# Second layers of group 1: two blocks through all their products, then the other two

## The chip, the cores and the metric

The kernel runs on one core of a Trainium2 chip. The metric is the time of one execution on the device in microseconds (us), as the median of several runs; lower is better.

## The reference

The program has two stages. The first is a gated linear recurrence over 768 steps for 4 x 8 heads of size 48; its output, with the heads side by side, is the matrix x of 3072 rows and 384 columns. The second is a mixture of four experts over the rows of x, and the change lies in its second layer:

```python
def _moe_ref(x, domain_probs, w1, w2):
    p = domain_probs / (domain_probs.sum(-1, keepdims=True) + 1e-09)
    out = np.zeros((N, D))                 # N, D, E, F = 3072, 384, 4, 1024
    for e in range(E):
        h = np.maximum(x @ w1[e], 0.0)
        out += p[:, e:e + 1] * (h @ w2[e])
    return out
```

## The kernel before

**Blocks and groups.** The rows of x are made in 24 blocks of 128 rows, called units, each by the generator `attention(u)` (lines 273 to 479). A group is a set of units that go through the experts together: group 0 has two units, groups 1 to 5 have four, group 6 has two. For every group and expert e the kernel runs `up` once for each of the eight f-chunks (fc, 128 of the 1024 hidden features) and then `down` for the group's blocks, here called slots. The two last groups take turns expert by expert; the others go one after the other.

**Split products.** A product of two fp32 matrices is made either whole, with fp32 operands, or from parts. Line 226 and the lines after it split a weight into a top, a low and a dif part, and lines 584 to 593 do the same for the hidden activations. A sum in parts is three products with fp32r operands: part 0 (H), part 1 (L) and part 2 (D), each taking the part of that number from weight and activation. In `up`, H and L go into one bank of PSUM ("one") and D into a second ("two"). In `down`, H and L of a slot go into one bank (`side` 0 of the code), and D into another (`side` 1), and each of the two sums is added into the slot's accumulator by `add_up`, on VectorE at line 666 (scaled by `p_fine` for side 0, by `p_all` for side 1) or, for the first sum of a slot, on ScalarE at line 664.

**Group 1.** Groups 2 and later split all of w1 and w2; they read the split weights from DRAM (`kept`), where group 0 put those of w1 and group 1 those of w2. Group 1 is in between. Its first layers use split w1. Its second layers use w2 whole for e = 0. For e = 1, 2 and 3 they use parts for the first half of the f-chunks (fc 0 to 3, w2 pieces 0 and 1, split during `up`), and the whole w2 for the other half (fc 4 to 7, pieces 2 and 3). These last are split only during and after the products, for the later groups. The whole products are part 3 in the code and are summed into the same bank as D.

**Order in `down`.** A call for group 1 with e > 0 takes all four slots, in two pairs. The steps, one matmul of 128x384 each, are written out as a list: line 613 runs over the sides, then the pairs, then the kinds of products of that side. That gives 64 steps: 16 H and L products of the first pair, 16 of the second, 8 whole and 8 D products of the first pair, 8 and 8 of the second. A sum gets its bank from a ring of four (pool tag "g", shared with "one" and "two" of `up`) at its first step, and its `add_up` is issued at its last.

Three things are tied to the number n of the step, not to the product that stands there: `background()`, which takes the next piece of work for splitting w2 (every eighth step); `make_dif` (line 592), which makes the dif part of the hidden activations of an f-chunk (at n = 3, 7, 11 and 15); and `advance`, which runs attention's next pieces when a clock of estimated costs has come to their due time. Every engine has its own queue and works through it in the order in which the instructions were issued.

**Names in the profile.** L637 is `down`'s matmul: "ops<-w,hT" is a product of parts, "ops<-hT" a whole product, of which each shows as two records. L538 and L546 are matmuls of `up`, L557 ScalarE's read of "one", L559 and L564 VectorE's read of "two" (L564 for the chunks that stay whole), L596 ScalarE's ReLU for these, L584, L586 and L592 the split of the hidden activations. L226 to L232 split w2, L502, L252 and L253 split x. Of attention, L270 is a transpose ("tp", of the inputs ra, rk, rq), read by L281, L286 and L293; L312 copies queries ("qb"); L338 and L393 are its score products ("sc", "far"), L348 and L406 take them up; L319, L321, L330 and L331 go to the next level.

Of the kernel before, what the change touches and what calls it, by code (L numbers as in the profile page):

```python
# [20 lines left out]
def kernel(  # L21
# [166 lines left out]
    def load_piece(l, i, beside=False):  # L188
        if i >= E * NQ * LAST:
            return  # L190
        gi, k = divmod(i, E * NQ)
        e, c = divmod(k, NQ)
        if gi > l:
            w = wt[l][i] = wts.tile([P, 3, KC * QF], F32R, name=f"w{l + 1}",
                                    bufs=AHEAD if l == 0 else NQ)
            nc.sync.dma_start(out=w.bitcast(F32), in_=kept[l][k])
            return
        if l == 1 and not beside:
            return
        if l == 0:  # L200

            if gi > 0 or e == 0:
                shared[c] = wts.tile([P, 3, KC * QF], F32R, name="w2", bufs=NQ)
            w = shared[c][:, 2 - e % 2 if gi == 0 else 2].bitcast(F32)
        else:

            place = (hidden[c][:, 0] if not split2(gi, e, c) else hidden[c + NQ // 2][:, 1])
            w = place.rearrange("p f n -> p (f n)")[:, :KC * QF].bitcast(F32)
        wt[l][i] = w
        if l == 0:  # L210
            heads = moe_w1[e].rearrange("(h d) f -> h d f", d=D)[:, :, c * QF:(c + 1) * QF]
            w = w.rearrange("p (c f) -> p c f", f=QF)
            for part in range(2):
                nc.sync.dma_start(out=w[:, part], in_=heads[part * H // 2:(part + 1) * H // 2, :QUAD])
            nc.sync.dma_start(out=w[:, 2], in_=heads[:, QUAD:])
        else:
            nc.sync.dma_start(
                out=w.rearrange("p (c d) -> p c d", d=DM),
                in_=moe_w2[e].rearrange("(c p) d -> p c d", p=P)[:, c * FPQ:(c + 1) * FPQ])

    def split_piece(l, i):
        whole = wt[l][i]
        w = wts.tile([P, 3, KC * QF], F32R, name=f"w{l + 1}", bufs=AHEAD if l == 0 else NQ)
        top, low, dif = (w[:, part] for part in range(3))

        nc.scalar.activation(out=top, in_=whole, func=ACT.Copy, scale=TRIM)  # L226
        yield
        nc.scalar.activation(out=dif, in_=whole, func=ACT.Copy, scale=TRIM * 4096)
        yield
        nc.vector.scalar_tensor_tensor(out=low, in0=whole, scalar=4096.0, in1=dif.bitcast(F32),  # L230
                                       op0=ALU.mult, op1=ALU.subtract)
        nc.vector.tensor_sub(dif, low.bitcast(F32), top.bitcast(F32))  # L232
        nc.gpsimd.dma_start(out=kept[l][i % (E * NQ)], in_=w.bitcast(F32))
        if l == 0:
            del wt[0][i]
        elif split2(1, *divmod(i - E * NQ, NQ)):
            wt[1][i] = w

    def background():


        for piece in list(splitting):
            if next(piece, splitting) is splitting:
                splitting.remove(piece)
        if making and len(splitting) < 4:
            splitting.append(making.popleft())
            next(splitting[-1])
# [343 lines left out]
    def make_dif(top, low, dif):  # L591
        nc.vector.scalar_tensor_tensor(out=dif, in0=top.bitcast(F32), scalar=1 / 4096.0,  # L592
                                       in1=low.bitcast(F32), op0=ALU.mult, op1=ALU.subtract)
# [5 lines left out]
    def down(gi, e, slots, between):  # L599


        first = first_piece(gi, e)
        in_parts = [fc for fc in range(FCH) if split2(gi, e, fc // FPQ)]
        whole = [fc for fc in range(FCH) if fc not in in_parts]
        if slots[0] == 0 and makes[1](gi, e):
            making.extend(split_piece(1, first + k) for k in range(NQ) if not split2(gi, e, k))
        if slots[0] == 0 and makes[0](gi, e) and 0 < e < E - 1:
            making.extend(split_piece(0, first + k) for k in range(2, NQ))


        pairs = [slots[k:k + 2] for k in range(0, len(slots), 2)]
        sides = [[((0, 1), in_parts[:-2]), ((0, 1), in_parts[-2:])], [((3,), whole), ((2,), in_parts)]]
        steps = [(side, slot, part, fc) for side in range(2) for pair in pairs
                 for parts, tiles in sides[side] for part in parts for slot in pair for fc in tiles]
        begins = {key: n for n, key in reversed([*enumerate(step[:2] for step in steps)])}
        ends = {step[:2]: n for n, step in enumerate(steps)}
        sums = {}
        for n, (side, slot, part, fc) in enumerate(steps):
            c, f = divmod(fc, FPQ)
            advance(cost(1, gi, e) * len(slots) / len(steps))  # L620
            while between and n >= between[0][0] * len(steps):
                between.popleft()[1]()
            if n and n % (len(steps) // (2 * len(slots))) == 0:
                background()
            if later and n % (len(steps) // 12 - 1) == len(steps) // 12 - 2:
                make_dif(*later.popleft())
            at = (side, slot)
            if n == begins[at]:
                sums[at] = ps.tile([P, DM], F32, name="ops", tag="g", bufs=4)
            h = hidden[c][:, :, f, slot * P:(slot + 1) * P]  # L630
            if part < 3:
                w = wt[1][first + c].rearrange("p t (c d) -> p t c d", d=DM)[:, part, f]
                h = h[:, part]
            else:
                w = wt[1][first + c].rearrange("p (c d) -> p c d", d=DM)[:, f]
                h = h[:, 2].bitcast(F32)
            nc.tensor.matmul(sums[at], lhsT=h, rhs=w, start=(n == begins[at]), stop=(n == ends[at]))  # L637
            if n == ends[at]:
                add_up(gi, e, slot, side, sums.pop(at))
        while between:  # L640
            between.popleft()[1]()
        background()
        if slots[-1] == len(groups[gi]) - 1 and gi != LAST - 1:
            while makes[1](gi, e) and (making or splitting):
                background()

            for c in range(NQ):
                del wt[1][first + c]
                if c < NQ // 2 or gi == LAST:
                    load_piece(1, first + NQ + c)  # L650
                else:
                    late.append(first + NQ + c)

    def add_up(gi, e, slot, kind, part):

        cb, b = groups[gi][slot]
        at = b * NCB + cb
        if e == 0 and (kind == 0 or not split2(gi, e)):
            accs[cb, b] = hid.tile([P, DM], F32, name="acc", bufs=B) if gi < LAST else \
                work.tile([P, NP * P], F32, name="QT")[:, :DM]  # L660
        acc = accs[cb, b]
        scale = (p_fine if kind == 0 else p_all)[:, at, e:e + 1]
        if e == 0 and (kind == 0 or not split2(gi, e)):
            nc.scalar.activation(out=acc, in_=part, func=ACT.Copy, scale=scale)
        else:
            nc.vector.scalar_tensor_tensor(out=acc, in0=part, scalar=scale, in1=acc,  # L666
                                           op0=ALU.mult, op1=ALU.add)
        if kind == 0:
            return
        if e == E - 1:  # L670
            del accs[cb, b]
            row = b * S + cb * P
            stores.append(lambda: (nc.sync if gi >= LAST - 1 else nc.gpsimd).dma_start(
                out=out[row:row + P, :], in_=acc))
# [3 lines left out]
    def cost(layer, gi, e):  # L678
        n = len(groups[gi]) / 4
        if layer == 0:  # L680
            return 2.1 * n if split1(gi, e) else 2.6 * n
        return 4.1 if gi > 1 else 4.7 if split2(gi, e) else 5.4
# [32 lines left out]
    def advance(spent):  # L715
        nonlocal clock
        clock += spent
        while waiting and clock >= waiting[0][0]:
            next(waiting.popleft()[2], None)

    with tc.manual_schedule():
# [38 lines left out]
        for fc in range(FCH):  # L760
            up(0, 0, fc, slice(0, 1))
            advance(cost(0, 0, 0) / 2)
        down(0, 0, [0], deque())
        while waiting:
            next(waiting.popleft()[2], None)
# [4 lines left out]
        for (gi, e), after in zip(tasks, [*tasks[1:], (None, None)]):  # L770
# [5 lines left out]
            turns = [range(k, k + each) for k in range(rest, len(groups[gi]), each)]  # L776
# [39 lines left out]
```

## Time and profile before

| | |
|---|---|
| Time, median of 9 runs | 1066.93 us (1066.0 to 1067.85) |
| Profiled execution | 1066.0 us, of which the span is 1064.2 us |
| Busy share of the span: PE, DVE, ACT, POOL | 98%, 73%, 53%, 3% |
| Chain of work that ended last: PE, ACT, DVE | 87%, 5%, 5% |
| `down`, products of parts | 1872 records, 347.5 us busy |
| `down`, whole products | 288 records, 101.0 us busy |
| Group 1's `down` with e = 1, 2, 3 | from 236.49, 282.06 and 326.73 us |

PE is TensorE, DVE is VectorE, ACT is ScalarE, POOL is GpSimd, SP is SyncE, which issues most DMAs. Times in rows of the profile are us from the start of the span, mean durations of one instruction are in ns. In a timeline each row has the start, the duration, the engine, the line, the operation, the tiles written and read, the number of records merged into it, and in brackets the engine's idle time before it with the instruction that ended that idle time.

### The profile page before, as it was taken

Reading aid. Unit: us, or ns where it says so; the run is one execution under the profiler, and the core shown is the slowest. Engines: PE = TensorE matmul, PEld = TensorE weight load, DVE = VectorE, ACT = ScalarE, POOL = GpSimd, SP = SyncE. Lnnn points to the kernel's source line nnn. Section 1 sums busy time; section 2 is a strip of 40 time slices with the busy share of each in tenths; the row PEclk is TensorE's granted clock in tenths of the full one; section 3 lists DMA queues with packets and bytes.
Section 4 is the critical chain, followed back from the end, with each engine's and each line's share of the span. In section 5 each row is a group of like instructions: output and inputs, shape, how many; then the busy total and the mean of one; then the engine's idle time right before and its main releaser. Section 6 shows DMA issues by size and latency. Waiting matters only on the chain.

```text
span 1064.2 us, 21598 instructions
## 1 busy us (share of the span) xinstructions
PE 1041.2 (98%) x8508; PEld 905.7 (85%) x8508; DVE 781.3 (73%) x1619; ACT 569.0 (53%) x1202; POOL 32.8 (3%) x71
## 2 busy tenths in 40 slices
PE   8899999999999999999999999999999999999998
PEld 8776776687877898898898998988989889898988
DVE  5488777667769777778877877986877875656565
ACT  5687876574655555536546535555464443323232
POOL 2010000000000000000000000000000000000000
PEclk9999999999999999999999999999999999999999
DMA  8597799896878958658659558585694454444531
GB/s 123 155 321 217 242 318 349 291 345 211 309 250 282 360 174 285 272 160 326 239 192 362 199 197 335 172 310 227 172 367 177 195 208 171 185 179 178 205 151 45
DMA packets 158837, 251.66 MB, mean 236 GB/s; under 512 B 120112, under 2 KB 135344, under 8 KB 136208
## 3 DMA queue, kind: packets, MB, share of 16 engines
q1 hardware_dynamic: 149600, 208.82, 57.5%
q0 software_dynamic: 5760, 41.29, 9.6%
q8 instruction: 67, 1.10, 0.4%
q10 hardware_dynamic: 3376, 0.17, 0.3%
q14 instruction: 34, 0.28, 0.1%
HBM read 207.79 MB, written 42.47 MB: 235 GB/s over the span
## 4 chain that ended last, share of the span: by engine, by line
PE 87%; ACT 5%; DVE 5%; issue 2%; DMA 1%; SPq 0%; DVEq 0%; ACTq 0%
PE ops L637 37%; PE one L546 22%; PE two L546 11%; PE sc L338 6%; PE yps L432 3%; PE tp L270 3%; PE one L538 2%; ACT qb L312 2%; PE far L393 1%; PE sps L467 1%; DVE near L348 1%; DVE w L230 1%; DMA rq<-in_q_dram 1%; ACT KT L330 1%; DVE QT L319 1%
## 5 line engine op out<-in xcount | busy, mean ns | idle before, releaser
L637 PE MATMUL ops<-w,hT 128*128 128x384 f32 x1872 | 347.5, 340 | 0.4 <-DVE hT L564 0.4
L637 PEld LDWEIGHTS ops<-w,hT 128*128 128x128 f32 x1872 | 325.3, 188 | 4.9 <-DVE hT L564 0.7
L546 PE MATMUL one<-xT,w 128*128 128x512 f32 x960 | 253.1, 399 | 2.2 <-DVE xT L252 1.4
L546 PEld LDWEIGHTS one<-xT,w 128*128 128x128 f32 x960 | 175.8, 188 | 41.3 <-DVE xT L252 3.1
L557 ACT ACTIVATE t<-one 128x512 f32<-128x512 f32 (+1 forms) x192 | 107.2, 558 | 183.9 <-PE one L546 178.6
L312 ACT COPY qb<-QT 64x256 f32<-64x256 f32 x336 | 136.6, 407 | 73.4 <-DVE QT L293 44.8
L586 DVE SCALAR_TENSOR_TENSOR hT<-t,hT 128x512 fp32r<-128x512 f32 (+1 forms) x172 | 110.5, 642 | 68.9 <-ACT hT L584 66.6
L559 DVE TENSOR_TENSOR t<-t,two 128x512 f32<-128x512 f32 (+1 forms) x172 | 109.4, 636 | 58.7 <-ACT t L557 29.7
L584 ACT ACTIVATE hT<-t 128x512 fp32r<-128x512 f32 (+1 forms) x172 | 101.8, 592 | 86.1 <-DVE t L559 85.0
L546 PE MATMUL two<-xT,w 128*128 128x512 f32 x480 | 136.3, 392 | 0.0
L546 PEld LDWEIGHTS two<-xT,w 128*128 128x128 f32 x480 | 90.1, 188 | 20.0 <-DVE acc L666 0.2
L637 PE MATMUL ops<-hT 128*128 128x384 f32 x288 | 101.0, 492 | 3.1 <-DVE acc L666 3.1
L592 DVE SCALAR_TENSOR_TENSOR hT<-hT 128x512 fp32r<-128x512 f32 (+1 forms) x172 | 100.9, 633 | 0.0
L348 DVE COPY_PREDICATED near<-masks,sc 128x256 f32<-128x256 uint8 x144 | 76.9, 534 | 19.3 <-PE sc L338 16.5
L319 DVE TENSOR_TENSOR QT<-QT,dec 128x256 f32<-128x256 f32 x144 | 60.8, 422 | 36.0 <-ACT qb L312 35.3
L338 PEld LDWEIGHTS sc<-qb,KT 128*64 128x64 f32 x2304 | 72.7, 138 | 9.3 <-issue 4.7
L338 PE MATMUL sc<-qb,KT 128*64 128x64 f32 x2304 | 77.2, 223 | 2.6 <-ACT qb L312 2.6
L637 PEld LDWEIGHTS ops<-hT 128*128 128x128 f32 x288 | 51.9, 190 | 32.5 <-DVE acc L666 3.7
L666 DVE SCALAR_TENSOR_TENSOR acc<-ops,p_all,acc 128x384 f32<-128x384 f32 x82 | 50.0, 614 | 32.4 <-PE ops L637 31.2
L330 ACT COPY KT<-KT 128x256 f32<-128x256 f32 x144 | 60.0, 417 | 3.1
L331 DVE TENSOR_TENSOR KT<-KT,dec 128x256 f32<-128x256 f32 x144 | 60.1, 418 | 0.0
L538 PE MATMUL one<-xT,w 128*128 128x256 f32 (+1 forms) x240 | 46.2, 340 | 0.6 <-ACT xT L448 0.6
(88 smaller groups left out, 935.0 us busy)
## 6 DMA issues: line engine op xcount, KB each, us to landing
w<-kept SPq DMA_DIRECT2D x144, 1152.0 KB
kept<-w POOLq DMA_DIRECT2D x32, 1152.0 KB, 7.3
hT<-in_moe_w_dram SPq DMA_DIRECT2D x32, 384.0 KB
w<-in_moe_w_dram SPq DMA_DIRECT2D x48, 128.0 KB
ra<-in_alpha_dram SPq DMA_DIRECT2D x23, 192.0 KB
rk<-in_k_dram SPq DMA_DIRECT2D x23, 192.0 KB
rq<-in_q_dram SPq DMA_DIRECT2D x23, 192.0 KB
out_dram<-acc POOLq DMA_DIRECT2D x18, 192.0 KB, 7.6
```

What stands on the lines that cost most here:

```text
L312: nc.scalar.copy(out=qb[rows, :, i, :].rearrange("p a (b r) -> p a b r", r=m), in_=qv[rows])
L319: nc.vector.tensor_mul(qv, qv, spread(dv[:, :, :, 0], m))
L330: nc.scalar.copy(out=new[:, :, :, 1, :], in_=old[:, :, :, 1, :])
L338: nc.tensor.matmul(out[HALF * s:HALF * (s + 1), 2 * p:2 * p + 2, :], lhsT=KTs[li][:, p, HALF * s:HALF * (s + 1)], rhs=qbs[li][:, p, :, QUA ...
L348: nc.vector.copy_predicated(near.rearrange("p a (b two r) -> p a b two r", two=2, r=m)[:, :, :, 1, :], mk.unsqueeze(1).broadcast_to([P, H, ...
L546: nc.tensor.matmul(out, lhsT=w[:, part, kc], rhs=x_part(gi, part, kc), start=(part == terms[0] and kc == 0), stop=(part == terms[-1] and k ...
L557: nc.scalar.activation(out=t, in_=one, func=ACT.Copy, scale=FINE)
L559: nc.vector.tensor_add(t, t, two)
L584: nc.scalar.activation(out=top, in_=x, func=ACT.Relu, scale=TRIM)
L586: nc.vector.scalar_tensor_tensor(out=low, in0=x, scalar=0.0, in1=top.bitcast(F32), op0=ALU.max, op1=ALU.subtract)
L592: nc.vector.scalar_tensor_tensor(out=dif, in0=top.bitcast(F32), scalar=1 / 4096.0, in1=low.bitcast(F32), op0=ALU.mult, op1=ALU.subtract)
L637: nc.tensor.matmul(sums[at], lhsT=h, rhs=w, start=(n == begins[at]), stop=(n == ends[at]))
```

## The change

Where a call of `down` has whole products beside products of parts, the pairs of slots become the outer loop and the sides the inner one. The first pair goes through H and L, whole products and D, and then the second pair does the same. Only the three calls for group 1 with e = 1, 2 and 3 have whole products and two pairs, so only their order differs. All other calls keep theirs. Lines after 613 have numbers higher by two.

```diff
         pairs = [slots[k:k + 2] for k in range(0, len(slots), 2)]
         sides = [[((0, 1), in_parts[:-2]), ((0, 1), in_parts[-2:])], [((3,), whole), ((2,), in_parts)]]
-        steps = [(side, slot, part, fc) for side in range(2) for pair in pairs
+        turns = [(side, pair) for pair in pairs for side in range(2)] if whole else \
+            [(side, pair) for side in range(2) for pair in pairs]
+        steps = [(side, slot, part, fc) for side, pair in turns
                  for parts, tiles in sides[side] for part in parts for slot in pair for fc in tiles]
```

## The prediction

> **What bounds the kernel now.** I read the page first: how busy is each engine, and what carries the chain that ended last?
>
> ```profile
> PE 1041.2 (98%) x8508; PEld 905.7 (85%) x8508; DVE 781.3 (73%) x1619; ACT 569.0 (53%) x1202; POOL 32.8 (3%) x71
> PE 87%; ACT 5%; DVE 5%; issue 2%; DMA 1%; SPq 0%; DVEq 0%; ACTq 0%
> ```
>
> TensorE (PE) is the bound. It idles for only 23 us of the 1064.2 us span, and an edit that moves no work off PE can win no more than the part of that idle time that it touches. So the second view is the busy time in the stretches of the three calls that the change reorders, those of down for group 1 with e = 1, 2 and 3. I took each stretch from the first H product to the first matmul of the next up. Columns: stretch, PE, PEld, DVE, ACT, POOL busy, clock, DMA share, GB/s.
>
> ```profile
> 236.49:260.31 23.82, 22.40 (x135) 17.10 (x135) 18.25 (x39) 10.99 (x23) 1.59 (x3) 1.00 0.78 249
> 282.06:304.78 22.72, 22.09 (x134) 17.00 (x132) 18.14 (x39) 9.86 (x20) 1.60 (x3) 1.00 0.81 261
> 326.73:350.48 23.75, 22.04 (x133) 17.02 (x132) 21.43 (x43) 12.62 (x27) 2.15 (x4) 1.00 0.88 294
> 350.50:450.00 99.50, 99.50 (x882) 88.58 (x882) 73.80 (x153) 53.27 (x113) 1.08 (x2) 1.00 0.73 270
> ```
>
> PE idles 23.82 - 22.40 = 1.42, then 0.63, then 1.71 us, 3.76 us in all. The two ups between the calls have PE busy for all of their 21.75 and 21.95 us, and after 350.5 us PE is busy without a gap, so whatever is won or lost by then reaches the end. The granted clock is 1.00 throughout.
>
> Third, PE's timeline: which wait is each gap?
>
> ```profile
> 241.69 1.84 PE L637 MATMUL ops<-w,hT 128*128 128x384 f32 x9
> 244.93 2.20 PE L637 MATMUL ops<-hT 128*128 128x384 f32 x6 [1.39 <-DVE acc L666]
> 285.70 1.15 PE L637 MATMUL ops<-w,hT 128*128 128x384 f32 x5 [0.36 <-DVE hT L564]
> 288.96 0.66 PE L393 MATMUL far<-qb,KT 128*64 128x128 f32 x8 [0.27 <-ACT qb L312]
> 335.07 2.85 PE L637 MATMUL ops<-hT 128*128 128x384 f32 x8 [1.71 <-DVE acc L666]
> ```
>
> The two large gaps stand at the same place: all 32 H and L products are done, and the first whole product wants a bank. The ring of four holds the sums of blocks 0 to 3, and block 0's is free only when VectorE (DVE) has added it up. Fourth, DVE's timeline around that place, in the first and in the second call:
>
> ```profile
> 243.54 0.68 DVE L592 SCALAR_TENSOR_TENSOR hT<-hT 128x512 fp32r<-128x512 f32 x1
> 244.25 0.62 DVE L666 SCALAR_TENSOR_TENSOR acc<-ops,p_fine,acc 128x384 f32<-128x384 f32 x1
> 244.79 0.68 DVE L592 SCALAR_TENSOR_TENSOR hT<-hT 128x512 fp32r<-128x512 f32 x1
> ...
> 290.03 0.61 DVE L666 SCALAR_TENSOR_TENSOR acc<-ops,p_fine,acc 128x384 f32<-128x384 f32 x1
> 290.56 0.68 DVE L592 SCALAR_TENSOR_TENSOR hT<-hT 128x512 fp32r<-128x512 f32 x1
> ```
>
> Block 0's products ended near 240, but its add-up starts at 244.25, behind splits and attention on a DVE that runs without a pause; 244.87 is when PE resumes. L592 makes the hidden dif, which the D products need; the fourth ends at 245.47, 291.24 and 335.61 in the three calls.
>
> **The change part by part.** Nothing is added or removed. In the program order of both kernels ACT, SP and POOL have the same instructions in the same order, DMAs included; on DVE the add-ups stay in their places and only change which sum they take. On PE the second pair's 16 H and L products go behind the first pair's 8 whole and 8 D products, and the transposes and scores of attention, tied to step numbers, fall at other products.
>
> Prices of a step from before's rows. H or L: twelve from 326.73 to the transpose at 328.83, so 0.18 us (0.19 in the first call). A whole product: 16 records of half a product from 253.75 to the next kind at 258.61, so 0.30 each, 4.86 us for a block of 8. D: eight from 258.61 to 260.31, 0.21. A transpose group: 0.36 to 0.44.
>
> *The bank wait goes.* The first pair's whole sums now take the ring's third and fourth bank, which hold the up's last "one" and "two". By the timelines of ACT and DVE, L557 and L564 have read those by 235.85 and 237.04 in the first call, 282.23 and 285.65 in the second, 326.90 and 328.19 in the third. PE reaches the whole products (16 x 0.19 plus a transpose) at 239.9, and (16 x 0.18, with or without a transpose) at 284.9 and 330.0. The fourth bank is first needed four products, 2.4 us, later. All are free. The second pair's H sums take the first two banks, whose add-ups end at 246.0, 291.8 and 336.1, while PE is there after 246.8, 292 and 336.9; its whole sums follow add-ups that end by 250.4, 295.8 and 340.6, wanted at about 252, 297 and 342. Gone: 1.39, 0.36 and 1.71 us.
>
> *The whole products come earlier*, at step 16 instead of 32. They need the hidden of the last f-chunk, made by ACT L596, which ends at 237.70, 286.31 and 328.85; the fourth whole product, three of 0.61 us after the first, is at 241.7, 286.7 and 331.8. That costs nothing, but in the second call the cover is only 0.4 us.
>
> *The D products come earlier: the new wait.* Before, D began at 250.33, 296.10 and 340.48, 4.9 us behind the fourth L592 each time. Now the D product that needs it, the fourth, stands at 239.9 + 4.86 + 0.4 + 3 x 0.21 = 245.8 in the first call, 284.9 + 4.86 + 0.36 + 0.63 = 290.8 in the second, 330.0 + 4.86 + 0.36 + 0.63 = 335.8 in the third. Against the three ends that is 0.3 us of cover, a wait of 0.4 (0.45 with the semaphore), and 0.2 of cover. From below the wait is 0 (a DVE that runs a little earlier); from above, each 1 us that DVE is later costs PE nearly 1 us in each call. Behind a PE that stands there wait the scores and transposes of attention. I take the worked values, the nearest rows: 0, 0.45, 0.
>
> *The moved attention steps.* In the second call far and its scores come after seven D products, at 292 instead of 288.96, so their 0.27 us wait for ACT's qb is gone; DVE L348, which reads the scores, stands at 294.07 and they end near 293.6: no cost, cover 0.4 us, and DVE has 2.43 us idle later in the call. The transpose of rk moves from 241.27 to about 244.3 and from 292.73 to 294.4; ACT L286 (244.09, 293.37) waits for it 0.6 and 1.5 us, with L228 and the lat copies queued behind. ACT then idles 7.32 and 3.63 us before its next copies of qb; DVE L230 at 247.38 wants L228, done by 246.2. Nothing on the path.
>
> *What is late next.* The third call ends in group 2's first up, whose third low part is DVE L252 at 348.83, ended at 349.51. DVE runs from 333.05 to 352.16 without a pause there, and the change takes nothing from its queue. PE, 1.71 us sooner, begins at 348.77 and wants that part after two matmuls of 0.23, at 349.23: a wait of 0.28, with the semaphore 0.35. The banks of the next sums (add-ups ended at 350.77 and 352.16) are wanted at 351.2 and 352.6, just covered.
>
> Sum: -1.39; -0.36 - 0.27 + 0.45 = -0.18; -1.71 + 0.35 = -1.36. In all -2.93 us. Made against the profiled execution, 1066.0 us with 1064.2 us of span, that is 1063.1; the median of the nine runs lies 0.93 us above that execution, so 1064.0 us, 0.27% less.
>
> A rule against it: the Trainium skill, TensorE: Matmul & The Clock Gate, Back-to-back issue gap, gives an isolated matmul N/2.4 + 2.5 ns at full clock, an estimated 162.5 ns at 384 columns. The rows have 180 to 190, beside weight loads of 188. By the rule the first pair would arrive at D 0.28 to 0.44 us sooner, all of it waiting for DVE, and the sum would be -2.4.
>
> **The rivals.** *The same: the gain is handed back at group 2* (chance 0.26). For: DVE has no pause from 333.05 to 352.16, and PE comes 1.7 us sooner to work that it feeds. If PE has to wait until DVE has drained, the third call's 1.71 is lost, and with a second-call wait of 0.45 there remain -1.57 us, 1065.4. Against: only one split and two banks are wanted in that time, each within 0.4 us.
>
> *Slower: D waits for dif* (0.08). Place: the first pair's fourth D, in each call. Its cover falls from 4.9 us to 0.3, -0.4 and 0.2. Should PE's stand there hold the transposes long enough for ACT, and so DVE's next L592, to fall behind, the wait feeds itself. The change comes out slower from where these waits exceed the worked ones by 2.93 us, 1 us a call; at 1.8 us a call it is +2.5 us, 1069.4. Against: in DVE's queue nothing ahead of the fourth L592 waits for a transpose that moved.
>
> That the change does not do what it says is excluded by the program order, which shows pair 0 through all parts and then pair 1 in all three calls, and in no other group.
>
> **How the numbers follow.** The forecast has 0.66. With all waits gone and none new the time is 1066.93 - 3.73 = 1063.2, and the runs spread by some 0.9 us about their median: low 1062.5. The high end takes in the rival that hands the gain back, with the same spread: 1066.5. Left out are the slower case and the ends of the others, under 2 in 10. A measurement of this kernel can tell about 0.2%, 2.1 us, from no change. The forecast clears that by 0.8 us, so faster has 0.66, same 0.26, slower 0.08.
>
> **What would show it.** Right: PE's waits name no L666 before whole products in the three calls; D in the second waits a few tenths on L592; the first "one" of group 2 waits for L252; the span is near 1061.3. Wrong: waits on L592 of over 1 us, a transpose that holds up ACT and then DVE, or a PE gap after 350 us that before does not have.

## The result and the profile after

The changed kernel takes 1062.51 us (median of 10 runs, 1060.75 to 1063.97) against 1066.53 us for the kernel before (30 runs): 4.0 us less, a ratio of 0.996 with a 95% interval of 0.9952 to 0.9968, that is 3.4 to 5.1 us. The direction is the one that was forecast. The size is not: 2.93 us was forecast, and the median lies at the very low end of the range of 1062.5 to 1066.5. The profiled execution took 1060.75 us with a span of 1059.0 us.

The three calls of `down` and the first up of group 2, from the profile after by stretches (columns: stretch, PE, PEld, DVE, ACT, POOL busy, clock, DMA share, GB/s):

```profile
236.23:258.12 21.89, 21.89 (x135) 17.21 (x134) 18.25 (x39) 10.97 (x23) 1.59 (x3) 1.00 0.83 268
279.97:302.19 22.22, 22.06 (x134) 17.06 (x133) 18.16 (x39) 9.78 (x20) 1.59 (x3) 1.00 0.81 262
324.20:345.95 21.75, 21.75 (x133) 17.06 (x132) 19.47 (x39) 11.49 (x25) 2.13 (x4) 1.00 0.82 285
345.95:368.43 22.48, 22.04 (x206) 18.08 (x205) 17.59 (x38) 14.76 (x31) 1.08 (x2) 1.00 0.98 394
```

The calls went from 23.82, 22.72 and 23.75 us to 21.89, 22.22 and 21.75: 1.93, 0.50 and 2.00 us less. Group 2's first up, which was 21.85 us long (350.48 to 372.33), is 0.63 us longer. "The stage" is, here and below, the time from the first H product of the first call to the start of group 2's attention outputs. In it PE's timeline of the changed kernel has only two gaps, those of the last two rows here:

```profile
239.59 4.68 PE L639 MATMUL ops<-hT 128*128 128x384 f32 x14
...
289.20 0.97 PE L639 MATMUL ops<-w,hT 128*128 128x384 f32 x4 [0.16 <-DVE hT L592]
...
347.03 1.19 PE L546 MATMUL one<-xT,w 128*128 128x512 f32 x4 [0.45 <-DVE xT L252]
```

The first row is the place of the old 1.39 us gap: the first whole products follow the H and L products at once. The second is the fourth D of the second call, waiting for its dif. The third is group 2 waiting for its third split of x. VectorE's rows show that its own pace did not change:

```profile
243.99 0.62 DVE L668 SCALAR_TENSOR_TENSOR acc<-ops,p_fine,acc 128x384 f32<-128x384 f32 x1
...
288.46 0.68 DVE L592 SCALAR_TENSOR_TENSOR hT<-hT 128x512 fp32r<-128x512 f32 x1
...
346.29 0.69 DVE L252 TENSOR_TENSOR xT<-x_raw,xT 128x512 fp32r<-128x512 f32 x1
```

Block 0's add-up starts 7.76 us after the first H product, as before (244.25 - 236.49). It is no earlier; it is no longer waited for.

What the timeline's brackets understate is seen in the waits of PEld, the loading of weights. First the kernel before, then the changed one, both from 225 to 375 us (columns: us in total, times, longest):

```profile
PEld ops L637 <- DVE acc L666: 3.7, 2, 2.0
...
PEld ops L637 <- DVE hT L564: 0.7, 1, 0.7
PEld far L393 <- ACT qb L312: 0.6, 1, 0.6
...
PEld tp L270 <- ACT AT L281: 0.3, 1, 0.3
```

```profile
PEld one L546 <- DVE xT L252: 0.9, 1, 0.9
...
PEld ops L639 <- DVE hT L592: 0.5, 1, 0.5
```

The same four gaps are 3.73 us in PE's brackets and 3.7 + 0.7 + 0.6 = 5.0 us here; after the change 1.4 us are left. The difference, 3.6 us, is also what the stage became shorter, but the match is not exact: the last row of the kernel before is a fifth wait, 0.35 us, that went with the change too, and the weight loads before far stand for 0.25 us where nothing is waited for. What each gap cost, from start to start, is worked out in the section on the prediction.

### The profile page after: what moved, and what is told of

It reads as the page before. It is cut to its first block, busy times and chain, and to the rows that moved or that the text cites. A ratio compares the mean times of both kernels' runs of the same rounds, so it can differ in the third digit from the quotient of the medians.

```text
span 1059.0 us, 21599 instructions
## 1 busy us (share of the span) xinstructions
PE 1039.3 (98%) x8508; PEld 904.9 (85%) x8508; DVE 781.0 (74%) x1619; ACT 568.8 (54%) x1202; POOL 32.8 (3%) x71
## 4 chain that ended last, share of the span: by engine, by line
PE 87%; DVE 5%; ACT 5%; issue 1%; DMA 1%; SPq 0%; ACTq 0%; DVEq 0%
PE ops L639 36%; PE one L546 23%; PE two L546 11%; PE sc L338 6%; PE yps L432 3%; PE tp L270 3%; PE one L538 2%; ACT qb L312 2%; PE sps L467 1%; PE far L393 1%; DVE near L348 1%; DVE w L230 1%; ACT KT L330 1%; DMA rq<-in_q_dram 1%; DVE QT L319 1%
## 5 line engine op out<-in xcount | busy, mean ns | idle before, releaser
L668 DVE SCALAR_TENSOR_TENSOR acc<-ops,p_all,acc 128x384 f32<-128x384 f32 x82 | 49.8, 614 | 29.6 <-PE ops L639 28.5
```

## The experiments

All stages below are measured alike: from the first H product of the first call to the next "up", the same for the other two calls, then the first up of group 2, and in the last column from that first H product to the attention outputs (yps) of group 2. All are differences of start times on PE's timeline, in us.

| kernel | call 1 | call 2 | call 3 | up of group 2 | whole stage |
|---|---|---|---|---|---|
| before | 23.82 | 22.72 | 23.75 | 21.85 | 126.97 |
| before again (e1) | 23.80 | 22.76 | 23.74 | 21.85 | 127.04 |
| changed | 21.89 | 22.22 | 21.75 | 22.48 | 123.33 |
| changed again (e9) | 21.89 | 22.22 | 21.75 | 22.51 | 123.36 |
| late dif (e2) | 22.18 | 22.73 | 23.16 | 22.86 | 125.94 |
| first call only (e3) | 21.89 | 22.74 | 23.74 | 21.74 | 125.04 |
| third call only (e4) | 23.80 | 22.75 | 21.75 | 22.50 | 125.71 |
| dif in up, new order (e5) | 21.87 | 22.04 | 22.50 | 23.55 | 124.80 |
| dif in up, old order (e6) | 23.36 | 23.30 | 26.38 | 21.85 | 129.72 |
| D before whole (e7) | 28.28 | 29.20 | 28.53 | 22.02 | 143.47 |
| one bank each (e8) | 30.48 | 31.27 | 32.64 | 21.73 | 151.05 |
| late dif, late x (e10) | 22.16 | 22.72 | 21.72 | 22.80 | 124.40 |
| new order, two moves (e11) | 21.89 | 21.72 | 21.77 | 22.13 | 122.45 |

The theory after the result (A): the gain is the bank wait of the first whole product, which came from a late add-up, less two new waits on VectorE's splits; and a gap costs about the time in which the weight loads stand. The rival (B): the new order itself, or something later in the span, makes a part of it.

### Each kernel once more

> The kernel before once more, for a second profile of it. Theory A (the gain sits in the three reordered calls and in the start of group 2): the three calls and the start of group 2 show the same gaps, in TensorE's weight loads 1.7, 0.7 and 0.6, and 2.0 us, and the distance from the first score products of group 2 (361.4 us in the first profile) to the end of the span varies by about 1 us from profile to profile without any change. Theory B (part of the gain is made after 850 us, where the changed kernel's profile drew 1.3 us further ahead): that distance is 702.8 us again, within 0.3 us, against the changed kernel's 701.5.

> The changed kernel once more, timed against before on the same chip and with a second profile. From the first H product of the first call to the attention outputs of group 2 it is 3.6 us shorter than before, as in its first profile, whichever theory holds. Theory A (all of the gain lies there; the last groups vary by 1 to 2 us from profile to profile): a ratio of 0.996 to 0.9975. Theory B (the last groups are shortened too): the rest of the span is again 1.3 us shorter than in the two profiles of before, and the ratio is 0.9955 or less.

Measured: the stage repeats within 0.1 us for either kernel, -3.6 us. The changed kernel again took 1063.79 us against 1066.7, a ratio of 0.9967 (0.9956 to 0.9978), -3.5 us in the middle, about what the stage has. (The medians differ by only 2.9 us. Six of these seven runs, but six of the twelve of the kernel before, have a mean granted clock of 0.998 and not 0.999 or 1.000; those with 0.998 alone average 1063.9 and 1067.7 us, 3.8 us apart.) The rest of the span, from the attention outputs of group 2 on, was 700.74 and 700.77 us before, and 699.44 and 699.90 after the change. So the two profiles of before agree as B expected, and the variation that A expected is not there; the ratio is in A's range. Over the other kernels this rest is 699.2 to 700.9 us. The new order in the third call mostly goes with the lower values, yet e7, which has it, gave 700.91, and e6, which does not, 699.74. The difference arises in the last two groups, after 850 us: up to there all these kernels are within 0.2 us of each other, counted from those outputs. Whether the change has a part in it, of 0.8 to 1.3 us, stays open.

### One call alone

```diff
-        turns = [(side, pair) for pair in pairs for side in range(2)] if whole else \
+        turns = [(side, pair) for pair in pairs for side in range(2)] if whole and e == 1 else \
```

In a second kernel the line has `e == 3`.

> The new order in the call with e = 1 alone. Theory A: that call loses its gap of 1.9 us with no new wait; the other two keep theirs; from the first H product of the first call to the scores of group 2 it is 1.8 us shorter than before. Theory B (what counts is PE's idle time as the profile prints it): 1.4 us shorter.

> The new order in the call with e = 3 alone. Theory A: the third call is 2.0 us shorter and the first up of group 2 waits about 0.6 us longer for the third split of x, so -1.4 us up to the scores of group 2. Theory B (group 2 hands the gain back, because VectorE has no pause): -0.5 us or less.

Measured: stage -1.93 and -1.26 us; 1064.27 and 1065.19 us in a single run each. The first is A's 1.8 and not the 1.4 of PE's printed idle time. In the third the call gained its 2.00 us in full, and group 2's first up gave back 0.65. The two leave 0.45 of the changed kernel's 3.64 us for the second call, which measures 0.50. The parts add up, and each call's gain is its own.

### The add-up's place in VectorE's queue

```diff
-            if later and n % (len(steps) // 12 - 1) == len(steps) // 12 - 2:
+            if later and (n >= 16 or not whole) and n % (len(steps) // 12 - 1) == len(steps) // 12 - 2:
```

> The order of the products stays as before; in the three calls the hidden dif splits are issued at steps 19, 23, 27 and 31 instead of 3, 7, 11 and 15, so they no longer stand in VectorE's queue ahead of the first pair's add-ups. Theory A (a gap is the add-up that comes late on VectorE, and its price is the time that the weight loads stand, 1.7 and 2.0 us): in the first call the add-up of block 0 ends near 243.0 and the gap goes, -1.9 us; in the third VectorE still waits for ScalarE's qb until 333.05, the add-up ends near 334.4, and 0.6 us of the gap goes; the second call keeps its gaps; -2.5 us in all, 1064.0. Theory B (the gain comes from the new order of the products itself, and of attention's steps between them): the order has not changed, so within 0.5 us of before.

Measured: 1066.03 us against 1065.92, a ratio of 0.9996 (0.9986 to 1.0005); stage -1.03 us. By the total this is B's result, though its interval, -1.5 to +0.5 us, holds the stage's -1.03 as well. By the stage A is right in the calls: -1.64 in the first, -0.59 in the third, with no change in the order of products. What A had not foreseen stands in the last columns: group 2's first up is 1.01 us longer. VectorE's rows say why:

```profile
334.25 0.43 DVE L319 TENSOR_TENSOR QT<-QT,dec 128x256 f32<-128x256 f32 x1 [1.77 <-ACT qb L312]
...
335.01 1.14 DVE L666 SCALAR_TENSOR_TENSOR acc<-ops,p_fine,acc 128x384 f32<-128x384 f32 x2
...
351.83 0.69 DVE L252 TENSOR_TENSOR xT<-x_raw,xT 128x512 fp32r<-128x512 f32 x1
```

In the third call the two early dif splits had filled most of a wait of VectorE for ScalarE's copy of qb. With the splits moved away, VectorE idles 1.77 us there instead of 0.60, and the moved splits now lie behind that wait. The third split of x starts 23.90 us after the call's first H product instead of 22.10. So the add-up waits for two things: VectorE's work ahead of it, and ScalarE.

> The old order of products, the dif splits at steps 19 to 31, and in the third call ScalarE's first split of x for group 2 at step 26 instead of 0. Theory A, refined (the add-up of block 0 comes when both are through: VectorE's work ahead of it, and ScalarE's copies of qb that attention's work ahead of it waits for): the gap of the third call goes too, since qb is ready near 331.3 instead of 333.0 and the add-up ends near 332.8, before PE's 333.2; first call -1.6, second 0, third -2.0 us, of which group 2's first up gives back 0.6 to 0.9: -2.9 us. Theory C (VectorE's work alone sets the add-up): the third call keeps -0.6, the whole -1.0 us as with the late dif splits alone.

The edit of the last kernel, and this one:

```diff
-                    for step, at in enumerate((0.0, 0.6, 0.7, 0.78)):
+                    for step, at in enumerate((0.4 if gi == 1 else 0.0, 0.6, 0.7, 0.78)):
```

Measured: 1064.04 us against 1066.7, 0.9968 (0.9955 to 0.9981); stage -2.57 us, of which the third call has -2.03, and group 2's first up gives back 0.95. Theory C, with VectorE's work alone, expected -0.6 in the third call. ScalarE no longer splits x ahead of its copies of qb, and VectorE's wait shrinks:

```profile
331.24 0.43 DVE L319 TENSOR_TENSOR QT<-QT,dec 128x256 f32<-128x256 f32 x1 [0.22 <-ACT qb L312]
...
332.00 1.14 DVE L666 SCALAR_TENSOR_TENSOR acc<-ops,p_fine,acc 128x384 f32<-128x384 f32 x2
```

Both gaps can thus be removed in the old order as well, by bringing the add-up forward. The new order does it by not needing the add-up.

### The dif splits in the up before

```diff
+        if gi == 1 and fc >= FCH // 2 and later:
+            make_dif(*later.popleft())
         background()
```

> The changed kernel, with the four hidden dif splits of each of the three calls issued one at a time in the last four f-chunks of the up before, not in the call. Theory A (what is left after the change are the wait of the fourth D on its dif in the second call, 0.5 us, and that of group 2's first up on the third split of x, 0.6 us, both because VectorE is late): VectorE is about 2 us less behind in the calls, the first wait goes and the second shrinks or goes, -0.5 to -1.1 us against the changed kernel, near 1061.6. Theory B (VectorE's work has only moved; the chunks of up then read their banks later, and PE waits there): no gain, or up to 1 us slower than the changed kernel.

> The kernel before, with only the same four splits moved into up; the order of the products stays as before. Theory A (add-ups late on VectorE make the gaps): the add-up of block 0 comes 0.7 to 2 us earlier, the gaps of the first and third call shrink from 1.9 and 2.0 us to 0.5 each or less, -2 to -3.4 us, 1063 to 1064.5. Theory B (the order of the products makes the gain): within 0.5 us of before.

Measured: in the new order 1065.2 us against 1066.78, 0.9982 (0.9973 to 0.9991), so slower than the changed kernel's 0.996; in the old order 1069.4 us, 1.003 (1.0019 to 1.0041), slower than before. A's expectation failed in both, and B's does not hold either: by the stage the one is 1.5 us slower than the changed kernel and the other 2.8 us slower than before, and PE does not wait in the two ups between the calls. In the third call of the old order the last hidden of up (VectorE L564) starts 2.54 us after the first H product, not 0.75: the splits stand ahead of it. ScalarE's ReLU and its copies of qb follow, and so does the add-up. One row each from the timelines of ScalarE, VectorE and PE:

```profile
330.39 0.63 ACT L598 ACTIVATE hT<-hT 128x512 f32<-128x512 f32 x1 [3.13 <-DVE hT L564]
```

```profile
335.21 0.43 DVE L319 TENSOR_TENSOR QT<-QT,dec 128x256 f32<-128x256 f32 x1 [1.77 <-ACT qb L312]
```

```profile
336.63 4.28 PE L639 MATMUL ops<-hT 128*128 128x384 f32 x8 [2.91 <-DVE acc L668]
```

At steps 3 to 15 the splits cost less, because there they lie partly in VectorE's own waits: in this kernel it idles 1.77 us for qb where it idled 0.60 us before.

### What the whole products and the banks are worth

```diff
-        sides = [[((0, 1), in_parts[:-2]), ((0, 1), in_parts[-2:])], [((3,), whole), ((2,), in_parts)]]
+        sides = [[((0, 1), in_parts[:-2]), ((0, 1), in_parts[-2:])], [((2,), in_parts), ((3,), whole)]]
```

> The changed kernel with each pair's D products ahead of its whole products. Theory A (the whole products are what covers the dif splits; they take 4.9 us): the first pair's fourth D waits for its split 5.0, 5.7 and 5.1 us in the three calls, and since banks stay free the rest is as in the changed kernel: 10 to 13 us slower than before, 1077 to 1080. Theory B (VectorE would catch up, since it only follows TensorE): under 3 us slower than before.

```diff
+        kept_sums = {}
...
-                sums[at] = ps.tile([P, DM], F32, name="ops", tag="g", bufs=4)
+                sums[at] = kept_sums[slot] if whole and in_parts and side else ps.tile([P, DM], F32, name="ops", tag="g", bufs=4)
+                kept_sums[slot] = sums[at]
```

> The changed kernel, but the whole and D products of a slot go into the same bank as its H and L products, after the add-up of these. Theory A (it is the free banks that make the new order faster): the first whole product of the first pair waits for the add-up of block 0, which ends 5.0, 5.8 and 5.1 us later than PE is there; the second pair waits up to 1 us; 11 to 16 us slower than before. Theory B (the order alone makes the gain, the add-ups follow TensorE): under 3 us slower than before.

Measured: 1084.85 and 1088.63 us in one run each, against a median of 1066.78: 18 and 22 us more, where A expected at most 13 and 16. B is out: VectorE does not catch up. In e8 PE stands at the first whole product for 4.92, 5.70 and 4.92 us, as worked out, and for 0.43, 1.26 and 2.52 us in the second pair, where up to 1 us was expected. In e7 the waits on dif begin with 2.41, 3.64 and 1.89 us and go on in smaller pieces, to 4.1, 4.5 and 3.7 us in all, less than the 5.0 to 5.7 expected. Both kernels lost more than these waits, since PE was also slower behind them:

```profile
245.02 7.50 PE L641 MATMUL ops<-hT 128*128 128x384 f32 x14 [4.92 <-DVE acc L670]
```

Fourteen records take 7.34 us to the transpose at 252.36, 0.52 each, where the changed kernel's need 0.32 (239.59 to 244.10). The cause is in the last section: the granted clock was 0.50 for 17 us of e7's stage and for 20 us of e8's.

### The two waits that were left

```diff
-            if later and n % (len(steps) // 12 - 1) == len(steps) // 12 - 2:
+            if later and (n == 12 if whole and n > 11 else n % (len(steps) // 12 - 1) == len(steps) // 12 - 2):
...
-                    for step, at in enumerate((0.0, 0.6, 0.7, 0.78)):
+                    for step, at in enumerate((0.0, 0.6, 0.7, 0.72 if gi == 1 else 0.78)):
```

> The changed kernel with two of VectorE's splits moved: the fourth hidden dif at step 12, ahead of the add-ups, instead of 15, and the third split of x for group 2 at step 47 instead of 50, ahead of one add-up and three steps of attention. Theory A (the two waits left are on these two splits, 0.5 and 0.6 us): both go, -1.1 us against the changed kernel's own run, -4.7 us against before. Theory B (VectorE has no pause, so whatever is put behind them is late instead: the add-ups that free the banks): within 0.3 us of the changed kernel.

Measured: stage -0.9 us against the changed kernel, -4.5 against before: the wait in the second call is gone (-0.50), that of group 2 costs 0.28 instead of 0.63 and is now on an add-up that was put behind the split. The time was 1062.82 us against 1066.7, 0.996 (0.9947 to 0.9973), beside 0.9967 (0.9956 to 0.9978) for the changed kernel on the same chip. The two intervals overlap; that this version is the faster one is shown by the stage, not by the total.

## Why the prediction was right in kind and wrong in size

**The place and the mechanism held.** The bank wait went in the first and third call, and no add-up (L666, now L668) ends a wait before whole products. The banks for the second pair were free in time. The whole products found their hidden ready. The moved transposes and scores cost nothing on PE. VectorE's and ScalarE's queues kept their pace: ScalarE's copies of qb behind the moved transposes start 16.37, 17.82 and 16.37 us after the first H product, against 16.37, 17.82 and 16.38 before. One reading was not exact: in the third call an add-up does change its place on VectorE, to behind the second split of x, without effect on the third.

**The step that failed is "Gone: 1.39, 0.36 and 1.71 us", with the 0.27 us of far.** It took PE's printed idle time for the price of a gap, and it left out a fifth wait. The printed time begins at the modelled end of the last matmul, which is 0.34 us long, while the next one would have started 0.18 us after it. So a gap between two products is about 0.16 us dearer, start to start. The first product behind it is also slower: behind the two large gaps the next record starts 0.43 us after the first, not 0.32. That makes 1.66 us in the first call and 1.98 in the third, where 2.00 went. In the second call the gaps on L564 and qb come to 0.63 and 0.34 us by start times.

The first call lost 0.25 us more, and that is the transpose of rk. The prediction moved it and counted nothing for it on the path, but in the kernel before its weight load had waited for ScalarE's copy L281:

```profile
241.27 0.42 PEld L270 LDWEIGHTS tp<-ident,rk 128*128 128x128 f32 x4 [0.35 <-ACT AT L281]
```

From the last product before it to the first behind it PE took 0.78 us, where the transpose of ra took 0.53. In the changed kernel it stands at 244.10 and does not wait. In e2 and e10, with the old order, the wait is there, and their first calls stay 0.29 and 0.27 us longer than the changed kernel's.

By the lengths of the calls 1.93, 0.98 (0.50 and the new wait's 0.48) and 2.00 us went, 4.91 in place of 3.73. So PE's idle time of 3.76 us, which the prediction took for a ceiling, was none. The low end of the range was built on the same 3.73 and was too high for the same reason. The range was also not what its own terms give: 1063.2 - 0.9 is 1062.3 and 1065.4 + 0.9 is 1066.3, not 1062.5 and 1066.5.

**The new waits.** D in the second call: 0.45 forecast, 0.48 in the weight loads. This estimate was made from start to start and held, with H products at 0.18 us (0.177 in the single records). With the 162.5 ns estimated from the Trainium skill, TensorE: Matmul & The Clock Gate, Back-to-back issue gap, it would have been 0.73. Group 2: 0.35 forecast, 0.63 measured; VectorE's split came when it was expected, 22.09 us after the call's first H product (22.10 before), and PE was there 0.3 us sooner than worked out, since the call had gained 2.00 and not 1.71. The two ups between the calls came out 0.10 and 0.06 us longer.

Together -4.91 + 0.48 + 0.63 + 0.16 = -3.64 us, the stage's difference. The median difference of 4.0 us has 0.4 us more, within its interval.

**The rivals.** That group 2 hands the gain back was right as a mechanism and had the right place (0.63 of 2.00 us); it did not grow to all of it, because only that one split was late: the banks were free when PE came. The slower rival, D on its dif, decides only where the whole products do not come first: e7 is that case, 18 us.

## What to carry to other kernels

Price a gap from start to start of the instructions around it, not by the idle time in brackets; the waits of the weight loads come nearer, and they name waits that the matmuls' own rows do not show. When a wait for a buffer comes from a consumer that runs late, an order of work that takes buffers which are already free can be worth as much as an earlier consumer, as in the third call here (2.00 and 2.03 us); what it then meets is the next thing that the same late engine makes, and that can be worked out from its rows. Work that looks movable may be filling another engine's wait: look at what its place hides before moving it.

## What was not expected of the hardware

Where PE stood for some microseconds the granted clock fell, so a long wait was paid twice. The third call of e6, in stretches around its gap of 2.91 us (columns as above; the clock is the last but two):

```profile
333.00:336.00 3.00, 0.73 (x5) 0.41 (x3) 1.23 (x5) 2.96 (x8) 0.00 (x0) 1.00 1.01 399
336.00:338.00 2.00, 1.37 (x2) 0.84 (x3) 1.10 (x3) 1.99 (x5) 0.00 (x0) 0.54 0.55 160
338.00:340.00 2.00, 2.00 (x5) 1.16 (x4) 1.66 (x5) 1.70 (x3) 0.00 (x0) 0.61 0.08 16
340.00:342.00 2.00, 2.00 (x10) 1.32 (x9) 1.97 (x3) 0.00 (x0) 0.00 (x0) 1.00 0.50 98
```

The eight records behind the gap start over 4.12 us (336.63 to the transpose at 340.75), against 2.68 us in the kernel before, whose gap of 1.71 us left the clock at 1.00. In e8, after 4.92 us, the clock was 0.50:

```profile
242.00:244.00 2.00, 0.00 (x0) 0.00 (x0) 2.00 (x6) 1.43 (x4) 0.00 (x0) 0.93 0.99 405
...
246.00:250.00 4.00, 4.00 (x8) 2.18 (x7) 3.34 (x7) 0.00 (x0) 0.06 (x1) 0.50 0.03 4
```

The Trainium skill, TensorE: Matmul & The Clock Gate, in its part on the HAM clock gate, gives half the clock after an idle window of about 3.4 us, and full clock after as long a busy one. The half agrees with these rows, and so do the slow stretches: 3.42 us in e6 (336.14 to 339.56), twice that in e8 (243.72 to 250.54).

The length of the gap does not agree, and by itself it does not decide in these runs. In e6 one of 2.91 us was enough, 3.25 us from the start of the last matmul before it to that of the first behind it; in e8 one of 2.52 us (to 368.12) left the clock at 1.00; and in the third call of e7 the clock fell behind one of only 1.89 us (to 345.79). What differs is how much PE worked in the 3.41 us ahead. First e7, then e8:

```profile
342.96:346.37 3.41, 1.42 (x9) 0.88 (x6) 2.82 (x7) 3.38 (x7) 0.00 (x0) 1.00 1.02 419
346.37:353.19 6.82, 5.01 (x13) 3.67 (x14) 6.29 (x13) 4.33 (x10) 0.00 (x0) 0.50 0.34 114
```

```profile
366.60:370.01 3.41, 1.89 (x6) 1.23 (x7) 3.38 (x8) 0.97 (x3) 0.00 (x0) 1.00 0.95 364
370.01:373.42 3.41, 3.41 (x12) 1.95 (x12) 0.87 (x2) 0.33 (x1) 0.00 (x0) 1.00 0.42 173
```

PE was busy for 1.42 us ahead of the fall in e7 and for 1.00 us in e6, and for 1.89 us in e8 without one. The limit is not sharp in these runs: near 167 to 170 us, ahead of the changed calls, the clock fell for 3.41 us in the profiles of e2, e7, e9 and e11 with 1.7 to 2.0 us busy. The gaps that the change removes lie close to it, with 2.01 and 1.67 us busy around the third call's gap in the two profiles of the kernel before. There the clock stayed at 1.00, so in these profiles their price is wait alone; whether it did in every other run is not shown.
